# Linear attention and an MLP mixer: attention on pairs of chunks, two-bank units, and an issue order planned in the kernel

## The chip, the cores and the metric

One core of a Trainium2 chip. The metric is the device time of one execution in microseconds (us).

Names: PE is TensorE (matmul), DVE is VectorE, ACT is ScalarE, POOL is GpSimd, SP is SyncE, which here only starts transfers. "ch1" and "ch2" are the two channel matmuls of the mixer, "tok1" and "tok2" the two token matmuls. PSUM is the memory, in banks, into which the matmuls of these kernels write; an eviction is the pass of VectorE or ACT that takes a result out of it. The granted clock is the share of its full clock that TensorE was given (PEclk in the views).

## The reference

Four batches, eight heads, 768 times, head size 48; then a mixer over times and channels.

```
f = 1 / (1 + exp(-f_logit))
for t in range(S):
    state = f[:, :, t, :, None] * state + outer(k[t], v[t])
    y[:, :, t] = q[t] @ state
x = y as [B, S, 384]
h = relu(x^T @ w_tok1) @ w_tok2            # 768 -> 256 -> 768, over times
u = x + h^T
out = u + relu(u @ w_ch1) @ w_ch2          # 384 -> 1536 -> 384, over channels
```

## The kernel before

It does attention one chunk of 128 times at a time. Gates are cumulative sums of log f, made by a matmul with a triangle; q and k are gated, transposed on TensorE, multiplied to scores, masked, and multiplied with v; a state is carried on. The mixing of batch b is cut into six slices, issued in the gaps of attention of batch b+1. Loads that also cast to bf16 are started by POOL:

```python
def load_batch_inputs(b, c0=0, c1=NCH):          # cut
    for c in range(c0, c1):
        nc.sync.dma_start(out=f_sb[i][:, :, c, :], in_=f_logit[b]...)
        nc.gpsimd.dma_start(out=q_sb[i][:, :, c, :], in_=q[b]...)   # and k, v
```

```python
# in attn_chunk(b, c); HP = 4 pairs of heads; cut
nc.vector.tensor_tensor(qh[i][:, :, 0:D], q_sb[ib][:, :, c, :], G[i][:, :, 0:D], ALU.mult)
nc.vector.tensor_tensor(kh[i][:, :, 0:D], k_sb[ib][:, :, c, :], Gi[i][:, :, 0:D], ALU.mult)
for hp in range(HP):
    nc.tensor.matmul(ps_AT[0][:, hp, :], lhsT=qb[:, hp, :], rhs=ident, start=True, stop=True)
for hp in range(HP):
    nc.tensor.matmul(ps_AT[1][:, hp, :], lhsT=kb[:, hp, :], rhs=ident, start=True, stop=True)
nc.scalar.copy(qkT[i][:, 0:4, :], ps_AT[0])
nc.vector.tensor_copy(qkT[i][:, 4:8, :], ps_AT[1])
# ... scores, mask, times v, state
```

```python
# in s_ch (ch1), evictions of 384 columns, one PSUM bank; cut
nc.tensor.matmul(pm[:, 0:384], lhsT=w_ch1[:, kt, cc * 128:(cc + 1) * 128],
                 rhs=uT[:, kt, th * 384:(th + 1) * 384], start=(kt == 0), stop=(kt == 2))
```

## Time and profile before

| kernel before | |
|---|---|
| time | 242.1 us median (242.0 to 242.7) |
| span of the profile | 240.4 us |
| TensorE busy, matmuls | 183.6 us, 1688 (by the weight loads; 15 matmul records are missing) |
| VectorE, ACT, POOL busy | 152.1, 137.2, 40.1 us |
| first ch1 matmul | 83.9 us |

The page of the kernel before: busy time, share of the span and instruction count of each engine, then TensorE's busy tenths in 40 slices of the span.

```profile
span 240.4 us, 4273 instructions
PE 183.6 (76%) x1673; PEld 111.5 (46%) x1688; DVE 152.1 (63%) x341; ACT 137.2 (57%) x262; POOL 40.1 (17%) x39
PE   0413376103858999999999999999999999989993
```

TensorE is nearly full from slice 14 on and mostly idle in the first ten. The table by stretches shows both stages; each row has the stretch, its length, and for each engine the busy time and the number of instructions, then the granted clock:

```profile
20.00:44.00 24.00, 11.86 (x108) 7.49 (x110) 17.75 (x32) 23.35 (x29) 10.84 (x8) 1.00 3.00 151
44.00:58.00 14.00, 0.70 (x12) 0.48 (x11) 1.06 (x3) 4.50 (x6) 5.67 (x6) 1.00 2.52 167
119.00:163.00 44.00, 41.99 (x417) 25.84 (x421) 34.51 (x83) 24.36 (x60) 1.39 (x1) 1.00 0.33 42
```

From 44 to 58 us TensorE does 0.7 us of work; later it does 42 of every 44. The chain that ended last (start, length, what) says what filled the head:

```profile
6.98 15.19 DMA q_sb_77<-in_q_dram
...
28.49 2.21 POOL k_sb_80 L78
30.70 11.26 issue
41.96 1.73 POOL v_sb_82 L79
44.17 13.95 DMA w_tok_73<-in_moe_w_tok_dram
```

POOL's queue holds the loads of batch 1 in front of the weights of the mixing. The load of v of batch 1 waits 11 us, so the weights are issued at 44 and are there at 58.

### The profile page before, as it was taken

The page shows a single profiled execution, that of the slowest core. Times are in us where ns is not written, and L with a number is a line of the kernel's source. Part 1 is how long each engine was busy: PE and PEld are TensorE (multiplying, and loading weights), DVE is VectorE, ACT ScalarE, POOL GpSimd, SP SyncE. Part 2 cuts the span into 40 slices and gives each one's busy share as a digit, 9 for nine tenths or more (in the row PEclk, how much of TensorE's full clock was granted, in tenths as well). Part 3 has the DMA queues.
Part 4 walks back from the last instruction along what each step waited for, and adds up shares of the span by engine and source line. Part 5 has one row for each costly group of instructions (what it writes and reads, how often), then busy time and mean ns, then how long its engine had stood idle before and what let it go on. Part 6 is the DMA issues. An engine that isn't in the chain of part 4 may idle for free.

```text
span 240.4 us, 4273 instructions
## 1 busy us (share of the span) xinstructions
PE 183.6 (76%) x1673; PEld 111.5 (46%) x1688; DVE 152.1 (63%) x341; ACT 137.2 (57%) x262; POOL 40.1 (17%) x39
## 2 busy tenths in 40 slices
PE   0413376103858999999999999999999999989993
PEld 0201253001535555566565555666556556546661
DVE  4323769300965999995489998637999872444221
ACT  5479999900697765870376777008776710556300
POOL 9823910821302100150300000000000000000000
PEclk9999999999965999999999999999999999999999
DMA  8999999999999900099490000121000002100022
GB/s 113 147 185 151 163 158 137 174 144 198 208 182 137 103 3 0 3 85 174 135 104 0 3 1 3 65 100 35 0 3 0 3 33 102 64 0 0 8 107 85
DMA packets 91539, 19.93 MB, mean 83 GB/s; under 512 B 80896, under 2 KB 91136, under 8 KB 91520
## 3 DMA queue, kind: packets, MB, share of 16 engines
q0 software_dynamic: 77168, 10.23, 78.3%
q1 hardware_dynamic: 14352, 9.44, 18.4%
q8 instruction: 13, 0.21, 0.4%
q14 instruction: 6, 0.05, 0.1%
HBM read 25.17 MB, written 4.72 MB: 124 GB/s over the span
## 4 chain that ended last, share of the span: by engine, by line
PE 34%; DVE 26%; DMA 15%; issue 9%; ACT 8%; POOL 7%; DVEq 0%; POOLq 0%
DMA q_sb_77<-in_q_dram 6%; DMA w_tok_73<-in_moe_w_tok_dram 6%; PE ps_moe_135 L298 5%; PE ps_moe_133 L298 5%; PE ps_moe_134 L298 5%; PE ps_moe_133 L280 3%; DMA out_dram<-out_sb_132 3%; DVE zT L285 3%; PE ps_moe_134 L280 3%; PE ps_moe_135 L280 3%; DVE u_nat L256 2%; DVE qkT_98 L186 2%; DVE AmT_99 L200 2%; DVE uT L270 2%; DVE state L225 2%
## 5 line engine op out<-in xcount | busy, mean ns | idle before, releaser
L298 PEld LDWEIGHTS <-zT 128*128 128x128 bf16 x288 | 27.7, 98 | 18.3
L280 PEld LDWEIGHTS <-w_ch_75 128*128 128x128 bf16 x288 | 26.5, 97 | 19.9 <-issue 4.5
L280 PE MATMUL ps_moe_133<-uT,w_ch_75 128*128 128x384 bf16 x96 | 22.9, 325 | 1.4 <-DVE uT L270 0.5
L280 PE MATMUL ps_moe_135<-uT,w_ch_75 128*128 128x384 bf16 x96 | 22.6, 325 | 0.8 <-DVE zT L285 0.5
L280 PE MATMUL ps_moe_134<-uT,w_ch_75 128*128 128x384 bf16 x96 | 22.2, 325 | 0.5 <-DVE zT L285 0.3
L220 ACT ACTIVATE x_nat_105<-ps_y 128x384 f32<-128x384 f32 x12 | 6.0, 499 | 24.8 <-PE ps_y L210 24.2
L298 PE MATMUL ps_moe_134<-w_ch_76,zT 128*128 128x384 bf16 x96 | 17.3, 326 | 0.0
L200 DVE TENSOR_TENSOR AmT_100<-ps_AT_122,tri_bf 128x512 bf16<-128x512 f32 x12 | 8.3, 688 | 14.2 <-PE ps_AT_123 L191 14.0
L298 PE MATMUL ps_moe_135<-w_ch_76,zT 128*128 128x384 bf16 x96 | 17.1, 326 | 0.0
L298 PE MATMUL ps_moe_133<-w_ch_76,zT 128*128 128x384 bf16 x96 | 17.1, 326 | 0.0
L287 ACT ACTIVATE zT<-ps_moe_134 128x384 bf16<-128x384 f32 x22 | 10.9, 496 | 8.0 <-PE ps_moe_134 L280 7.8
L161 PE MATMUL ps_dg<-ones_bf,Lhi_85 128*128 128x1 bf16 x40 | 3.5, 166 | 13.5 <-ACT Lhi_85 L143 6.7
L287 ACT ACTIVATE zT<-ps_moe_135 128x384 bf16<-128x384 f32 x22 | 11.0, 500 | 4.9 <-PE ps_moe_135 L280 4.8
L220 ACT ACTIVATE x_nat_104<-ps_y 128x384 f32<-128x384 f32 x12 | 5.8, 486 | 13.9 <-PE ps_y L210 13.9
L247 PE MATMUL ps_moe_134<-x_bf_106,w_tok_73 128*128 128x384 bf16 x6 | 2.5, 452 | 14.1 <-DMA w_tok_73<-in_moe_w_tok_dram 12.2
L247 PEld LDWEIGHTS <-w_tok_73 128*128 128x128 bf16 x48 | 4.6, 105 | 17.9 <-DMA w_tok_73<-in_moe_w_tok_dram 12.4
L287 ACT ACTIVATE zT<-ps_moe_133 128x384 bf16<-128x384 f32 x20 | 10.0, 500 | 4.3 <-PE ps_moe_133 L280 4.2
L224 DVE TENSOR_TENSOR state<-state,ps_dg 48x192 f32<-48x192 f32 x20 | 6.8, 342 | 8.5 <-ACT qkT_98 L185 4.9
L257 ACT ACTIVATE u_bf<-u_nat 128x384 bf16<-128x384 f32 x24 | 11.0, 519 | 1.8 <-DVE u_nat L256 1.6
L200 DVE TENSOR_TENSOR AmT_99<-ps_AT_122,tri_bf 128x512 bf16<-128x512 f32 x12 | 8.2, 685 | 6.0 <-PE ps_AT_123 L191 5.7
L175 ACT ACTIVATE glast<-ps_dg 128x4 f32<-128x4 f32 x20 | 3.6, 178 | 14.1 <-DVE state L227 12.7
L191 PE MATMUL ps_AT_122<-qkT_97 48*128 48x128 bf16 x48 | 5.1, 232 | 7.3 <-ACT qkT_97 L185 5.5
(149 smaller groups left out, 470.3 us busy)
## 6 DMA issues: line engine op xcount, KB each, us to landing
out_dram<-out_sb_131 SPq DMA_DIRECT2D x12, 192.0 KB, 1.9
out_dram<-out_sb_132 SPq DMA_DIRECT2D x12, 192.0 KB, 1.9
f_sb_83<-in_f_logit_dram SPq DMA_DIRECT2D x6, 192.0 KB, 5.7
q_sb_78<-in_q_dram POOLq DMA_DIRECT2D x2, 576.0 KB, 12.6
k_sb_80<-in_k_dram POOLq DMA_DIRECT2D x2, 576.0 KB, 18.2
v_sb_82<-in_v_dram POOLq DMA_DIRECT2D x2, 576.0 KB, 11.6
w_ch_75<-in_moe_w_ch_dram POOLq DMA_DIRECT2D x1, 1152.0 KB, 20.3
w_ch_76<-in_moe_w_ch_dram POOLq DMA_DIRECT2D x1, 1152.0 KB, 24.9
```

The source lines that it names most:

```text
L186: nc.vector.tensor_copy(qkT[i][:, 4:8, :], ps_AT[1])
L191: nc.tensor.matmul(ps_AT[par][:, hp, :], lhsT=qkT[i][rows, 4 + hp, :], rhs=qkT[i][rows, hp, :], start=True, stop=True)
L200: nc.vector.tensor_tensor(AmT[i][:, 0:4, :], ps_AT[0], tb4, ALU.mult)
L220: nc.scalar.activation(x_nat[ib][:, c, :], yflat, AF.Copy, bias=0.0, scale=1.0)
L224: nc.vector.tensor_tensor(state[0:D], state[0:D], ps_dg[0:D, :, 0:D], ALU.add)
L225: nc.vector.tensor_tensor(state[64:64 + D], state[64:64 + D], ps_dg[64:64 + D, :, D:2 * D], ALU.add)
L247: nc.tensor.matmul(pm[:, 0:DM], lhsT=w_tok1[:, kt, rt * 128:(rt + 1) * 128], rhs=x_bf[ib][:, kt, :], start=(kt == 0), stop=(kt == NCH - 1))
L257: nc.scalar.activation(u_bf[:, stt, :], u_nat[:, stt, :], AF.Copy, bias=0.0, scale=1.0)
L280: nc.tensor.matmul(pm[:, 0:384], lhsT=w_ch1[:, kt, cc * 128:(cc + 1) * 128], rhs=uT[:, kt, th * 384:(th + 1) * 384], start=(kt == 0), stop ...
L285: nc.vector.tensor_scalar(dst, pm[:, 0:384], 0.0, None, ALU.max)
L287: nc.scalar.activation(dst, pm[:, 0:384], AF.Relu, bias=0.0, scale=1.0)
L298: nc.tensor.matmul(pm[:, 0:DM], lhsT=zT[:, kt, tt * 128:(tt + 1) * 128], rhs=w_ch2[:, kt, :], start=(kt == 0), stop=(kt == 11))
```

## The change

The intent: half as many small instructions in attention (times 2p and 2p+1 on partition p, so one cumulative sum serves two chunks), passes of 768 or 1024 columns over two PSUM banks instead of 384 or 512, transposes on the DMA engines instead of TensorE for q, k and u of batches 1 to 3, fp32 loads on SP's queue with the casts on POOL, and one order for everything. That order is made by a planner inside the kernel: every operation has an assumed duration and a priority; the planner simulates the engines, picks engine and buffer greedily, and issues in the order that it found. Each engine then runs its instructions strictly in that order. The diff, cut to its core (constants, imports and most of the planner left out):

```diff
+LD_ISSUE, ROW = 0.8, 0.019 / 16
+class Planner:
+    # greedy: of the ready operations, the one with the earliest start, then the
+    # lowest prio; (occupancy, latency) of each engine it may run on is given
+    ...
+                    cand = [s for s in self.pools[p] if s[1] is not None and s[1] <= st + 1e-9]
+                    s = max(cand, key=lambda s: s[1])
+XB_FROM = 1
-        nc.gpsimd.dma_start(out=q_sb[i][:, :, c, :], ...)
+        P.op(f"ld{nm}{b},{d}", {"SP": (LD_ISSUE, 0)}, [], [f"{nm}{b},{d}"],
+             lambda: nc.sync.dma_start(out=P[f"{nm}{b},{d}"]..., in_=src[d]), ...)
-    nc.gpsimd.dma_start(out=w_tok2, in_=moe_w_tok2.rearrange("(kt p) n -> p kt n", p=128))
+    P.op("w2", {"DVE": (1.0, 0.1)}, ["w2s0", "w2s1"], ["w2"], lambda: [nc.vector.tensor_copy(
+        w_tok2[:, kt].rearrange("r c (two p) -> r c p two", two=2), ...) for kt in range(2)], -898)
+            nc.gpsimd.tensor_copy(o[0:64, 0:2], x[0:64])          # v cast, one of four
-    for hp in range(HP):
-        nc.tensor.matmul(ps_AT[0][:, hp, :], lhsT=qb[:, hp, :], rhs=ident, start=True, stop=True)
+        xbar = b >= XB_FROM
+        if not xbar:
+            # batch 0: 16 transposes of a pair on TensorE, evicted 1024 columns at a time
+            ...
+        else:
+            for e in range(2):
+                P.op(f"xb_t{i},{e}", {"ACT": (0.8, 0)}, [f"qh{i}", f"kh{i}"], [f"qkT{i},{e}"],
+                     lambda e=e: nc.scalar.dma_start_transpose(
+                         P[f"qkT{i}"][:, 1024 * e:1024 * (e + 1)]..., P[f"qh{i}"][64 * e:64 * e + 64]),
+                     pr - 500, xfer=-1.1)
+            # u, batches 1 to 3:
+                P.op(f"uT{i}", {"ACT": (1.0, 0)}, [f"ub{i}"], [f"uT{i}"],
+                     lambda i=i, p=p: nc.scalar.dma_start_transpose(...), p_tok - 500, xfer=-0.8)
+    for s, _, o, e in P.order:       # issue in the planned order
+        o.fn(e)
```

The numbers in parentheses after an engine are the durations that the planner assumes: 0.8 us of ACT for starting a q/k transpose, 1.0 for one of u, 0.8 of SP for a load.

## The prediction

> **What bounds the kernel now.** Two stages. Until 58.2 us nothing of the mixing runs. The chain of waits shows why: q/k/v pieces issued one after another from POOL (about 0.9 us each, a 15.2 us DMA step), an 11.3 us "issue" wait in POOL's queue behind the batch-1 loads, then w_tok1, issued at 44.2 and landed 13.9 us later. The table by stretches gives PE 16.3 us busy of the first 58. From 58 to 237 TensorE is the limit: 41.5 to 42 us busy of each 43 to 44 us per batch, DVE 34 to 36, ACT 24. (58 to 76 also ran at a granted clock of 0.76.) From matmul spacing in the timeline (0.163 us at 384 columns, 0.22 at 512, 0.055 for a 128-column transpose, 0.026 to 0.045 for the small ones) TensorE needs about 27.4 us per batch for the mixing and 2.4 us per chunk for attention: 170 us in all, 156 of them in those 179 us, so 87% used. After that stage only a 0.55 us add and a store remain.
>
> **What the change does.**
> 1. Attention on pairs of times: half the cumulative sums, gate sums and score/AV groups. I count 2.1 to 2.4 us TensorE per two chunks instead of 4.8. Transposes of q/k (batches 1 to 3) and u go to DMA. TensorE total: 109 mixing + 27 attention + 4 transposes of batch 0 = 140 us, 30 less.
> 2. Two-bank evictions of 768 or 1024 columns. From the trace a DVE pass costs 0.15 us + 1.04 ns per column, ACT 0.19 + 0.83 ns, so DVE about 127 us of 152. ACT about 80 us of 137, plus 27 transpose issues of 1 to 1.7 us that hold its queue; the nine act-table loads of 1.28 us become one.
> 3. Casting loads leave POOL: q/k/v/f are fp32 on the SP queue with 384-byte rows instead of 192; POOL casts v, state and x. w_tok1 is issued once k of the second pair landed, not after batch 1.
> 4. Planned order interleaves attention b+1 with mixing b.
>
> **On the critical path.** Head: twelve 393 KB loads at 1.3 to 2.5 us each, first pair's chain about 15 us after f lands at 4, then DVE bound in batch 0 (about 8.5 us per pair by the formula above) for two more pairs: x complete near 36, tokens, u and its transpose near 43 instead of about 81. Only about 16 us of TensorE work is done by then. The remaining 124 us, at about 93% use, take 134. Tail 3.5: a 0.95 us add, two stores. Sum about 180 of span; the time reads 1.7 us above the span.
>
> **Prediction: 181 us, 8 in 10 between 171 and 195.** Faster by over 2%: 0.97; within 2%: 0.02; slower: 0.01.
>
> **What would show it.** First ch1 matmul at 40 to 46 us; TensorE at least 90% busy from there to the end; TensorE matmul count 1514; no DMA wait for weights over 3 us; DVE around 125 us busy, ACT 80.
>
> **What would make it wrong.** DMA transposes: no trace here has one. The Trainium skill, "DMA: Bandwidth & Descriptors", Latency and other measured facts, puts them at 261 GB/s, so 1 us per 256 KB is an estimate; slower ones, or ACT held while issuing, delay scores and ch1 (u's transposes sit between tokens and channels in every batch). POOL as caster: "SBUF — State Buffer", Who interferes with whom, says a DVE instruction with two SBUF inputs blocks GpSimd reads; the gates are such, and POOL produces v and state. Loads and weights (11 MB) competing at the start could push ch1 past 50. A fixed order that guesses durations wrongly makes engines wait in line. All push up; better interleaving pushes to 172.

## The result, and the profile after

The kernel after takes 234.1 us median (232.6, 232.7, 235.5, 235.6). The ratio to the kernel before is 0.965, 95% interval 0.959 to 0.971. Ratios in this document compare the runs of two kernels in the same rounds, and are not quite the ratio of the medians quoted. It is faster, and 53 us slower than predicted, far outside the range.

| | before | predicted | after |
|---|---|---|---|
| time, us | 242.1 | 181 | 234.1 |
| TensorE matmuls | 1688 | 1514 | 1514 |
| first ch1, us | 83.9 | 40 to 46 | 58.0 |
| VectorE busy, us | 152.1 | 125 to 127 | 145.1 |
| ACT busy, us | 137.2 | 80 and 27 issues | 90.4 and 49.4 of issues |

The page of the kernel after, as that of before:

```profile
span 230.7 us, 3882 instructions
PE 172.3 (75%) x1514; PEld 101.9 (44%) x1514; DVE 145.1 (63%) x221; ACT 90.4 (39%) x130; POOL 84.0 (36%) x134
PE   0455726585976859948828999929998999799990
PEclk9999999999795999995965999988999999999998
DMA  7999999999897999979990330693435004711052
```

TensorE starts earlier but then has holes (a 4, two 2s, a 7 after the first third), where before it was at 9 throughout; between slices 11 and 28 the granted clock falls at times as well. The table by stretches of the kernel after (same columns as before):

```profile
60.00:80.00 20.00, 15.66 (x146) 8.27 (x145) 15.47 (x25) 13.77 (x21) 9.22 (x15) 0.77 1.06 214
80.00:100.00 20.00, 17.23 (x164) 10.29 (x163) 16.19 (x20) 8.32 (x13) 15.00 (x21) 1.00 1.03 203
100.00:120.00 20.00, 11.51 (x119) 6.40 (x118) 12.19 (x18) 5.66 (x8) 4.87 (x9) 0.75 1.04 194
140.00:160.00 20.00, 15.78 (x132) 8.85 (x130) 12.01 (x23) 5.81 (x10) 5.05 (x10) 0.91 0.52 83
200.00:220.00 20.00, 20.00 (x125) 12.05 (x124) 5.74 (x6) 6.49 (x8) 0.00 (x0) 1.00 0.13 32
```

From 100 to 120 no engine computes for more than 61% of the time: TensorE 11.5 of 20, VectorE 12.2, ACT 5.7. ACT's queue is held by issues for about 11 more, which the table does not count as busy. This is not a load that is too big but engines waiting for one another. The transfers (what, who starts them, how many, KB each where known, median us from issue to landing):

```profile
qkT<-qkh ACTq DMA_TRANSPOSE x18, 4.7
uT<-u_bf ACTq DMA_TRANSPOSE x9, 2.8
```

ACT's own timeline from 99 us on shows what such a transpose does to it. ACTq is ACT's queue held by an issue, not ACT computing; in brackets the idle time before and what ended it:

```profile
98.99 3.12 ACTq L421 DMA_TRANSPOSE qkT<-qkh  x2
102.16 0.81 ACT L377 ACTIVATE G<-pp 128x768 bf16<-128x768 f32 x1 [7.01 <-issue]
102.87 0.81 ACT L379 ACTIVATE Gi<-pp 128x768 bf16<-128x768 f32 x1
103.56 0.84 ACT L346 ACTIVATE f_ld<-f_ld 128x768 f32<-128x768 f32 x1
104.44 0.84 ACT L348 ACTIVATE f_ld<-f_ld 128x768 f32<-128x768 f32 x1
105.19 0.79 ACT L533 ACTIVATE h1T<-pp 128x768 bf16<-128x768 f32 x1
105.87 4.50 ACTq L421 DMA_TRANSPOSE qkT<-qkh  x2
```

The gate exponentials of line 377 stand behind two transposes. At 145 us four transposes in a row hold ACT for 7.7 us, and TensorE's token matmul waits 4.2 us for the eviction that stands behind them (the last line is TensorE's timeline):

```profile
145.47 7.67 ACTq L421 DMA_TRANSPOSE qkT<-qkh  x4
153.18 0.81 ACT L533 ACTIVATE h1T<-pp 128x768 bf16<-128x768 f32 x1 [7.68 <-issue]
154.04 1.10 PE L548 MATMUL pp<-h1T,w_tok 128*128 128x384 bf16 x4 [4.22 <-ACT h1T L533]
```

The issue of one q/k transpose took (minimum, median, maximum in ns, then first and last start):

```profile
L421 ACTq DMA_TRANSPOSE qkT<-qkh x18: 1257/1758/3676, 57.6 to 172.7; - x18
```

The planner assumes 800. The pieces of ACTq in the timeline sum to 49.4 us. SP is touched too: the waits of SP's queue have its loads waiting for transposes, because in the compiled program the transfers of SP and ACT take eight completion semaphores in turn, and a transfer waits until an earlier user of its semaphore has landed (what waited, for what: us in total, times, longest):

```profile
SPq L258 <- DMA qkT<-qkh: 27.2, 5, 7.5
```

So there are three suspects in the transposes: ACT held while it issues, the time to landing that the scores wait for, and the traffic and semaphores shared with the loads. The chain of waits of this kernel has all of them. Two landings stand in it:

```profile
80.54 8.19 DMA qkT<-qkh
107.16 5.27 DMA qkT<-qkh
```

Landings of q/k transposes are 5.8% of this chain (13 us) and their issues on ACT 3.8% (9 us).

The head is a second loss. Up to 58 us VectorE is busy 44.4 us, and 17.8 of the 20 between 20 and 40. The loads do not hold it: the only one in the chain of waits before 58 us is the first of f, 3.9 us. Two things on VectorE took longer than estimated, the two copies that permute w_tok2 (planner: 1.0 us for both) and the gates, and batch 1's gates had a bad place in the order:

```profile
L288 DVE COPY w_tok<-zT x2: 2240/2388/2537, 26.2 to 28.0; 128x768 bf16<-128x768 bf16 x2
```

```profile
53.69 1.65 DVE L398 TENSOR_TENSOR qkh<-q_ld,G 128x384 bf16<-128x384 f32 x2
55.26 2.27 DVE L398 TENSOR_TENSOR qkh<-k_ld,Gi 128x384 bf16<-128x384 f32 x2
57.45 0.94 DVE L576 CAST uT<-pp 128x768 bf16<-128x768 f32 x1
```

The second fence is VectorE's timeline just before the first ch1: the last eviction of batch 0's transposed u, which ch1 needs, stands behind the gates of batch 1. TensorE had made that transpose by 55.5.

### The profile page after: what moved, and what is told of

The parts are those of the page before. It is cut to its first block, busy times and chain, and to the rows that moved or that the text cites. A ratio compares the mean times of both kernels' runs of the same rounds, so it can differ in the third digit from the quotient of the medians.

```text
span 230.7 us, 3882 instructions
## 1 busy us (share of the span) xinstructions
PE 172.3 (75%) x1514; PEld 101.9 (44%) x1514; DVE 145.1 (63%) x221; ACT 90.4 (39%) x130; POOL 84.0 (36%) x134
## 3 DMA queue, kind: packets, MB, share of 16 engines
q10 hardware_dynamic: 26208, 6.49, 19.2%
## 4 chain that ended last, share of the span: by engine, by line
PE 41%; DVE 19%; DMA 15%; ACT 9%; issue 8%; ACTq 4%; POOL 1%; SPq 0%; DVEq 0%; POOLq 0%
PE pp L595 15%; PE pp L626 12%; DVE qkh L398 7%; DMA qkT<-qkh 6%; DVE AmT L454 4%; ACTq L421 4%; PE pp L548 3%; DMA q_ld<-in_q_dram 3%; DMA out_dram<-xu 3%; PE pp L528 2%; PE pp L451 2%; DVE state L493 2%; DMA uT<-u_bf 2%; ACT xu L510 2%; ACT f_ld L346 2%
## 5 line engine op out<-in xcount | busy, mean ns | idle before, releaser
L595 PE MATMUL pp<-uT,w_ch 128*128 128x384 bf16 x288 | 58.6, 348 | 5.9 <-ACT zT L606 2.2
L626 PE MATMUL pp<-w_ch,zT 128*128 128x384 bf16 x288 | 57.2, 331 | 2.1 <-ACT xu L510 1.9
L595 PEld LDWEIGHTS <-w_ch 128*128 128x128 bf16 x288 | 28.0, 103 | 26.9 <-issue 11.0
L606 ACT ACTIVATE zT<-pp 128x768 bf16<-128x768 f32 x31 | 24.7, 813 | 32.3 <-PE pp L595 27.4
L454 DVE TENSOR_TENSOR AmT<-pp,msk 128x1024 bf16<-128x1024 f32 x24 | 28.9, 1220 | 9.7 <-PE pp L451 9.4
L506 POOL CAST state_bd<-state 48x192 bf16<-48x192 f32 x40 | 15.8, 396 | 34.4 <-DVE state L496 27.5
L608 DVE TENSOR_SCALAR zT<-pp 128x768 bf16<-128x768 f32 x17 | 16.3, 957 | 15.3 <-PE pp L595 11.7
L638 DVE TENSOR_TENSOR xu<-xu,pp 128x768 f32<-128x768 f32 x12 | 11.4, 949 | 19.0 <-PE pp L626 19.0
L554 DVE TENSOR_TENSOR xu<-xu,pp 128x768 f32<-128x768 f32 x12 | 11.2, 952 | 13.6 <-PE pp L548 13.6
L398 DVE TENSOR_TENSOR qkh<-q_ld,G 128x384 bf16<-128x384 f32 x24 | 15.1, 670 | 4.3 <-ACT G L377 4.3
L398 DVE TENSOR_TENSOR qkh<-k_ld,Gi 128x384 bf16<-128x384 f32 x24 | 17.7, 776 | 0.0
L302 POOL CAST x_bf<-xu 128x768 bf16<-128x768 f32 x10 | 8.5, 846 | 25.3 <-ACT xu L510 22.6
L451 PEld LDWEIGHTS <-qkT 48*128 48x128 bf16 x192 | 7.2, 110 | 16.2 <-issue 8.7
```

Of the source, the lines that this page charges most:

```text
L398: nc.vector.tensor_tensor(gated(z, nm, j), x[:, j], gg[:, j], ALU.mult)
L451: nc.tensor.matmul(A[:, par, hp], lhsT=qkT(1, hp, e, rows), rhs=qkT(0, hp, e, rows), start=True, stop=True)
L454: P.op(f"mk{ic}", {"DVE": dve_t(1024)}, [f"A{ic}"], [f"Am{ic}"], lambda ic=ic: nc.vector.tensor_tensor(P[f"Am{ic}"], P[f"A{ic}"].rearrange ...
L506: nc.gpsimd.tensor_copy(P[f"bd{ic}"][r, :, cl], P[f"st{ic}"][r])
L595: nc.tensor.matmul(pm[:, th, 0:384].rearrange("p (a t) -> p a t", t=128), lhsT=w_ch1[:, kt, cc * 128:(cc + 1) * 128], rhs=uT[:, 3 * th:3 * ...
L606: nc.scalar.activation(o, x, AF.Relu)
```

## The experiments

The theory: the DMA transposes cost the time between the first ch1 and the end, by holding ACT and by landing late. The rivals: it is not the transposes but an order made from wrong durations, whatever the operation; buffers handed out too soon; or the head alone, whose delay the rest only carries on.

All kernels are built from the kernel after by the edit shown. The planner runs again in each, so where durations or engines are edited the order on all engines changes too; where that is not so, it is said. Every run gave a correct result and was timed in three rounds. They were timed in five sets on five chips; the median of the kernel before lay between 242.2 and 242.9 us in all of them. Two more builds never ran, because the greedy planner found no order: a2 with the planner told that SP issues the transposes, and d1 without the later priority of the copies.

| run | time, us (median) | ratio to before | 95% interval |
|---|---|---|---|
| after | 234.1 | 0.965 | 0.959 to 0.971 |
| a1_no_xbar | 218.0 | 0.898 | 0.895 to 0.901 |
| a2_sp_xbar | 226.8 | 0.935 | 0.932 to 0.939 |
| a3_fifo | 230.0 | 0.947 | 0.945 to 0.950 |
| a4_replan | 224.4 | 0.923 | 0.919 to 0.926 |
| b1_u_xbar | 218.0 | 0.898 | 0.895 to 0.901 |
| b2_w2_on_act | 216.6 | 0.893 | 0.891 to 0.895 |
| b3_v_on_act | 222.0 | 0.914 | 0.912 to 0.917 |
| n1_null | 233.1 | 0.961 | 0.955 to 0.967 |
| c1_dummy_xbar | 239.3 (mean of three) | 0.988 | 0.981 to 0.995 |
| c2_dummy_on_sp | 224.4 | 0.925 | 0.921 to 0.929 |
| c3_hold_act | 236.4 | 0.971 | 0.966 to 0.976 |
| d1_costs_tensor | 215.1 | 0.889 | 0.887 to 0.891 |
| d2_costs_u_dma | 212.0 | 0.875 | 0.873 to 0.877 |
| d3_costs_fifo | 213.8 | 0.883 | 0.880 to 0.885 |
| d4_best_fifo | 212.7 | 0.878 | 0.873 to 0.882 |
| e2_ev_on_act | 211.1 | 0.870 | 0.866 to 0.874 |

### a1: all transposes on TensorE

```diff
-    XB_FROM = 1
+    XB_FROM = 4
```

> All transposes of batches 1 to 3 (q, k and u) back on TensorE with evictions on ACT and DVE; the planner makes a new order. Theory 1 (the DMA transposes, 49 us of ACT's queue and 4.7 us median to landing, cost most of the missing 50 us): TensorE gets about 11 us more work and still the kernel gets faster, 205 to 222 us. Theory 2 (early reuse of buffers, and waits between queues): 230 to 240. Theory 3 (DVE and POOL slower than planned by contention): 235 or more, since DVE gets more work.

Measured: 218.0 us, 16 under the kernel after, with 198 matmuls more. The page of a1, TensorE's line and its slices:

```profile
PE 174.3 (81%) x1712; PEld 109.7 (51%) x1712; DVE 148.8 (69%) x224; ACT 114.1 (53%) x157; POOL 81.7 (38%) x131
PE   0456536659668689979987999999899999999990
PEclk9999999999979999999999999999999999999999
```

The holes after 100 us are gone and the clock is at full speed but for one slice. The DMA transposes took more than the TensorE work they were to save. First ch1 is at 58.7, as before the edit: the head has nothing to do with them.

### b1: only q and k back on TensorE

```diff
-        xbar = b >= XB_FROM
+        xbar = False
```

> Only the nine u transposes stay DMA transposes; q and k are transposed on TensorE in all batches. If the 18 q/k transposes are the cost (34 us of ACT's queue, scores wait for them): near the kernel without any, 215 to 221 us. If the u transposes between tokens and channels cost as much: 222 to 230.

Measured: 218.0 us, the same as a1. So the nine transposes of u by DMA cost nothing net in this plan; the 18 of q and k are the whole difference.

### a2: the transposes issued from SP

```diff
-  nc.scalar.dma_start_transpose(        # both places
+  nc.sync.dma_start_transpose(
```

The order on TensorE, VectorE and POOL is exactly that of the kernel after.

> The same plan and order on PE, DVE, ACT and POOL, only the 27 transposes are issued by SP instead of ACT. If it is the time ACT is held while issuing (49 us in all): 210 to 222 us. If it is the latency of the transposes or the plan: 228 to 238, and the loads and stores behind them in SP's queue may come later.

Measured: 226.8 us; 7 of the 16 us came back. The waits of a2 show where the rest went: the loading of score weights, and the score matmuls, wait for the transposes, up to 10 us at a time.

```profile
PEld L451 <- DMA qkT<-qkh: 18.8, 6, 10.2
PE pp L451 <- DMA qkT<-qkh: 16.6, 4, 9.8
```

SP's queue is in order as well, so transposes and loads now hold each other up there. This run alone cannot divide the cost.

### a3: buffers taken first in, first out

```diff
-                    s = max(cand, key=lambda s: s[1])
+                    s = min(cand, key=lambda s: s[1])
```

The order on all engines is that of the kernel after; only which buffer is used changes.

> Same order on every engine; only the choice of a free buffer is changed from the most recently freed to the longest free. Theory 2 (ACT at 116 us waits for a store of a tile that was reused although others were free, loads wait for just-used tiles): 220 to 228 us. Theories 1 and 3: 230 to 235.

Measured: 230.0 us. Taking the buffer freed last, which the planner believes free, makes 4 us of waits where its times are wrong: a small term.

### a4: the planner told what the trace shows

```diff
-    LD_ISSUE, ROW = 0.8, 0.019 / 16
+    LD_ISSUE, ROW = 1.4, 0.019 / 16
-    P.op("w2", {"DVE": (1.0, 0.1)}, ...
+    P.op("w2", {"DVE": (4.4, 0.1)}, ...
-                P.op(f"xb_t{i},{e}", {"ACT": (0.8, 0)}, ...
+                P.op(f"xb_t{i},{e}", {"ACT": (1.8, 0)}, ...
-                P.op(f"uT{i}", {"ACT": (1.0, 0)}, ...
+                P.op(f"uT{i}", {"ACT": (1.3, 0)}, ...
```

> Same instructions, replanned with the issue times that the trace shows: 1.8 us per q/k transpose, 1.3 per u transpose, 1.4 per load, 4.4 for the w_tok2 permutation. If a fixed order made from wrong durations is the loss: 212 to 225 us. If the transposes cost in themselves: 226 to 236.

Measured: 224.4 us, 10 us better with the same operations. So part of the loss is that the order was made with wrong durations. This run corrects four of them at once, so it does not show how much of the 10 us belongs to that of the q/k transposes, told at less than half the true one. And it is not the whole loss: a4 is still 6 us above b1, which kept the wrong durations and only took the q/k transposes off the DMA engines.

### n1: a shuffled plan, nothing else

A changed plan could be better or worse by luck. This run changes one assumed latency and thereby the order.

```diff
-PE_LAT = 0.10
+PE_LAT = 0.15
```

> A control: the changed kernel with one planner constant nudged (0.10 to 0.15 us), which shuffles the order without making it truer. Says how far any new order moves the time. 230 to 237 us if the order is not the matter; outside that, differences of that size between replanned kernels prove nothing.

Measured: 233.1 us, within the spread of the kernel after. This shuffle moved the time by about 1 us, so gains of 10 and 16 are unlikely to be luck. It is one shuffle only; a difference of 3 us between two plans is less safe.

### c1, c2, c3: which part of a q/k transpose costs

All three are a1 (the scores read transposes made by TensorE) plus something that nobody reads. They share one plan, and the order on TensorE, VectorE and POOL is the same in all three (c2 has one more memset at the start).

```diff
# c1: 18 DMA transposes into unread tiles, started by ACT
+    P.op(f"xb_t{i},{e}", {"ACT": (0.8, 0)}, [f"qh{i}", f"kh{i}"], [],
+         lambda e=e: nc.scalar.dma_start_transpose(dummy..., P[f"qh{i}"][64 * e:64 * e + 64]), ...)
# c2: the same from SP, reading a fixed tile: traffic only
+         lambda e=e: nc.sync.dma_start_transpose(dummy[0]..., dummy[1][64 * e:64 * e + 64]), ...)
# c3: ACT held by a copy of 1900 columns: no transfer
+         lambda e=e: nc.scalar.copy(dummy[e][:, 0:1900], P[f"qh{i}"][:, 0:1900]), ...)
```

> As a1 (scores read q/k transposed by TensorE), plus the 18 q/k DMA transposes of batches 1 to 3 issued from ACT into tiles that nobody reads. a1 read 218.0. If the cost of the q/k transposes is that they hold ACT's queue (18 times about 1.8 us) and slow the loads, this run keeps it: 225 to 232, with ACT-queue steps in the chain of waits and PE waiting for ACT evictions. If the cost is that the scores wait for the transposes' results (4.7 us to land), this run loses it: 218 to 221. From the run with the transposes on SP (7 of 16 us gone) I expect between: about 224, and no PE wait on DMA qkT.

Measured: 239.3 us (mean of three runs, 237.2 to 240.5). My expectation of 224 was wrong: nobody waits for the results any more, and the whole cost is still there and more, 21 us over a1. The wait of the scores for the landing is therefore not needed to explain it.

> c1 with the 18 unread DMA transposes issued from SP and reading a fixed tile, so they hold no ACT and wait for no data; order on PE, DVE and POOL is that of c1. What is left of them is their traffic and their time and semaphores in SP's queue among the loads. If that was c1's cost: 232 to 239. If holding ACT was it: 218 to 222. I expect 221.

Measured: 224.4 us, 6 over a1. Traffic, SP's time, semaphores and the different plan cost that much together.

> c1 with each of the 18 unread DMA transposes replaced by an ACT copy of 1900 columns (about 1.75 us by the copies in the trace) into an unread tile: ACT is held as long as by a median issue, no transfer, no DMA semaphore. If the bare holding of ACT is the cost: 230 to 238. If the cost of the issues is their waiting in ACT's queue for a DMA completion semaphore still in use by a load, or the transfers: 219 to 224. I expect about 228.

Measured: 236.4 us, 18 over a1, without a single transfer. A copy takes 1776 ns (c3), an issue 1800 in median (c1, slow run):

```profile
L405 ACT COPY dummy<-qkh x18: 1758/1776/1779, 57.9 to 179.5; 128x1900 bf16<-128x1900 bf16 x18
```

```profile
L405 ACTq DMA_TRANSPOSE dummy<-qkh x18: 1257/1800/3211, 57.0 to 182.6; - x18
```

Holding ACT for that time, 18 times, at places where the plan left 0.8 us, is most of the cost: c1 is 15 us above c2, and c3, without any transfer, is 12 above c2, which has the same plan, and 18 above a1, which has another. Holding here includes standing in the queue: in c3 ACT also waited 7.0 us, four times, for the gates that the copy reads, and nothing waited for the copies' results. ACT is busy only 58% of c3's span, so it is not overloaded. What it does next is late, and everything behind stands in order. The table by stretches, a1 first and then c3:

```profile
58.00:100.00 42.00, 35.61 (x378) 21.89 (x377) 38.97 (x60) 30.68 (x45) 26.20 (x39) 0.96 0.94 205
```

```profile
58.00:100.00 42.00, 34.33 (x338) 20.83 (x339) 35.29 (x50) 34.75 (x43) 26.22 (x39) 0.80 0.68 154
```

TensorE started 378 matmuls in this stretch in a1 and 338 in c3, and both VectorE and TensorE are less busy. TensorE's granted clock is lower too, 0.80 against 0.96, so a part of the loss comes through the clock. A caveat: in c1 and c3 ACT also evicts TensorE's transposes, which it doesn't in the kernel after. So these are shares in c1, not measured in the kernel after.

### b2 and b3: the head

b2 is a1 with the two w_tok2 copies on ACT at the same place in the order; b3 also puts the v casts of batch 0 on ACT instead of POOL.

```diff
# b2
-    P.op("w2", {"DVE": (1.0, 0.1)}, ..., lambda: [nc.vector.tensor_copy(
+    P.op("w2", {"DVE": (1.0, 0.1)}, ..., lambda: [nc.scalar.copy(
# b3, in addition
-            nc.gpsimd.tensor_copy(o[0:64, 0:2], x[0:64])      # and three more
+            cp = nc.scalar.copy if b == 0 else nc.gpsimd.tensor_copy
+            cp(o[0:64, 0:2], x[0:64])
```

> The kernel without DMA transposes (217.97 us), same order on all engines, only the two permuting copies of w_tok2 (2.39 us each on DVE, in the DVE-bound head, beside POOL's casts) are issued on ACT. If the head is DVE bound and they lie on its path: 3 to 5 us less, 213 to 215. If the head waits for something else: 217 to 219.

Measured: 216.6 us, 1.4 under a1, first ch1 at 56.4 instead of 58.7. On ACT the two copies took 7.1 us and held up an eviction that TensorE waited 3.9 us for, with VectorE behind it (2.9 us), so most of the gain was probably given back there.

> As the last, and in batch 0 the four casts of v per pair go from POOL to ACT, same order. If POOL's reads slow DVE's two-input instructions (gates 0.67 to 0.97 us where 0.5 is seen alone): gates in the first 58 us fall to 0.55 and the kernel gains 2 to 4 us more, 209 to 213. If ACT then lies on the path: 214 to 218.

Measured: 222.0 us, worse than b2 by 5: a miss. But it settles one thing. The timelines of VectorE, the gates of batch 0's first two pairs, b2 and then b3:

```profile
10.16 1.65 DVE L398 TENSOR_TENSOR qkh<-q_ld,G 128x384 bf16<-128x384 f32 x2 [0.29 <-ACT G L377]
11.74 1.95 DVE L398 TENSOR_TENSOR qkh<-k_ld,Gi 128x384 bf16<-128x384 f32 x2
20.02 1.16 DVE L398 TENSOR_TENSOR qkh<-q_ld,G 128x384 bf16<-128x384 f32 x2
21.10 1.79 DVE L398 TENSOR_TENSOR qkh<-k_ld,Gi 128x384 bf16<-128x384 f32 x2
```

```profile
10.14 1.03 DVE L399 TENSOR_TENSOR qkh<-q_ld,G 128x384 bf16<-128x384 f32 x2 [0.29 <-ACT G L377]
13.92 1.03 DVE L399 TENSOR_TENSOR qkh<-k_ld,Gi 128x384 bf16<-128x384 f32 x2 [2.75 <-ACT Gi L379]
21.27 1.02 DVE L399 TENSOR_TENSOR qkh<-q_ld,G 128x384 bf16<-128x384 f32 x2
22.21 1.02 DVE L399 TENSOR_TENSOR qkh<-k_ld,Gi 128x384 bf16<-128x384 f32 x2
```

Two gates take 1.02 us when POOL is not casting and up to 1.95 when it is. The Trainium skill, "SBUF — State Buffer", Who interferes with whom, has VectorE and GpSimd share one pair of ports under an exclusive lock; these lines agree that casts slow the gates, and do not show a lock as such. In b3 ACT held the head up instead: TensorE waited 6.3 us at one place for an eviction behind the copies and casts on ACT, and VectorE 6.7 us behind it.

### d1 to d4: combinations

d1 is a1 with the measured durations (1.4 us per load issue, 4.4 us for w_tok2's copies) and the copies at a priority behind batch 0's masks. d2 is d1 with u's transposes by DMA (1.3 us told), q and k on TensorE. d3 and d4 are d1 and d2 with buffers first in, first out.

```diff
# d2 against the kernel after
-    LD_ISSUE, ROW = 0.8, 0.019 / 16
+    LD_ISSUE, ROW = 1.4, 0.019 / 16
-    P.op("w2", {"DVE": (1.0, 0.1)}, ..., -898)
+    P.op("w2", {"DVE": (4.4, 0.1)}, ..., 62)
-        xbar = b >= XB_FROM
+        xbar = False
-                P.op(f"uT{i}", {"ACT": (1.0, 0)}, ...
+                P.op(f"uT{i}", {"ACT": (1.3, 0)}, ...
```

> All transposes on TensorE as in a1, planner told the measured 1.4 us per load issue and 4.4 us for the two w_tok2 copies, which also get a priority behind batch 0's mask passes (in the planner 62 instead of -898). If mis-told durations still cost time without any DMA transpose: 213 to 216. If a1's remaining loss is only work (DVE in the head): 217 to 219. First ch1 at 55 to 57 against 58.7 in a1.

> The same measured costs, q/k on TensorE, the nine u transposes by DMA and told at 1.3 us. b1 read the same as a1, so theory says the same as d1 within 1 per cent: 212 to 217. TensorE count about 1658.

> d1 with the buffer that was freed longest ago taken instead of the one freed last; instruction order as d1. The same change was worth 4 us in the after kernel, where buffers were held by late transposes. If buffer reuse makes engines wait without them too: 2 to 4 us under d1; if it only mattered for late transposes: within 1 us of d1.

> d2 (q/k on TensorE, u by DMA, measured durations; 212.0) with the buffer freed longest ago taken, which was worth 1.3 us on d1. 210 to 212 if the same here.

Measured: d1 215.1, d2 212.0, d3 213.8, d4 212.7. Measured durations, with the copies placed later, are worth 3 us on a1 and 6 on b1. The buffer rule is worth 1.3 us on d1 and nothing on d2. d2 is 3 us under d1: with q and k on TensorE, moving u's transposes to the DMA engines may gain a little, though the plans differ and b1 gained nothing on a1. It is 9% under the kernel after and 12.5% under the kernel before.

### e2: less work for VectorE

In d2 VectorE is busy 42.1 of the 44.5 us from the first ch1 to 100 us (the third figure with a count):

```profile
55.50:100.00 44.50, 38.88 (x422) 23.88 (x419) 42.09 (x63) 31.17 (x46) 25.95 (x39) 0.98 1.06 221
```

e2 lets only ACT evict the transposed q/k of batches 1 to 3.

```diff
-  P.op(f"ev{z}{i}", {"ACT": act_t(1024), "DVE": dve_t(1024)}, ...
+  P.op(f"ev{z}{i}", {"ACT": act_t(1024)} if b else {"ACT": act_t(1024), "DVE": dve_t(1024)}, ...
```

> d2 with the evictions of transposed q/k of batches 1 to 3 allowed on ACT alone; VectorE gets about eight instructions fewer, some 8 to 10 us. If VectorE, not TensorE, limits the stretch from the first ch1 to about 100 us (39.8 of 42 us busy in d2): TensorE use rises there and the time falls by 2 to 5 us, to 207 to 210. If TensorE or ACT limits it: within 1.5 us of 212.

Measured: 211.1 us; the interval of its ratio overlaps that of d2, so it isn't shown to be faster. It is also a poor test: VectorE lost 8.5 us over the whole span, but only 1.8 of them in the stretch in question. That VectorE limits this stretch remains a reading of the table, not a result.

## Why the prediction was wrong

The busy time of TensorE is no measure of work: a ch1 matmul lasts 0.326 us in the trace, but back to back they start every 0.1625 us. For the sums below, work is the number of matmuls of each kind in a stretch times the spacing that the trace shows when they run back to back (0.1625 us for 384 columns, 0.055 for a transpose, 0.0255 to 0.042 for the small ones).

**The work was right.** Predicted 140 us in all, 16 before the first ch1 and 124 after it. Counted in the trace of after: 16.2 and 125.5. The matmul count, 1514, was exact. The sum, 141.7, is within 2 us of the prediction.

**The head: 43 predicted, 58.0 measured (+15).** The step that failed is "x complete near 36, tokens, u and its transpose near 43". The last x of batch 0 was complete near 45.7: VectorE, which I had named as the limit, had 4.8 us of permuting w_tok2 that I had left out, and gates and sums slowed by POOL's casts (in b2's trace the six pairs of gates of batch 0 sum to 8.6 us where 6 times 1.03 would be 6.2). I had cited the port rule as a risk and given it no microseconds. From 45.7 to 58 instead of 7 us it took 12, with the gates of batch 1 in front of the last eviction. No run shows that these terms are the 15 us: with the copies elsewhere, b2 and d1 bring the first ch1 only to 56.4 and 55.6, so the cause of most of the head's loss stays open. VectorE's total, 145 instead of about 126, comes in part from the same terms: the 48 gates took 32.8 us, 6 more than at 0.55 us each; w_tok2 adds 4.8; the sums of line 350 averaged 0.79 us. The remainder I have not divided.

**The stage: 134 us at 93% use predicted, 166.7 measured (+33).** From 58.0 to the last matmul's end at 224.7, 125.5 us of work is 75% use. The step that failed is "The remaining 124 us, at about 93% use, take 134", through the term "27 transpose issues of 1 to 1.7 us that hold its queue", which I had added to ACT's load and not to any wait. The issues took 49.4 us of ACT's queue, 1.8 each in the mean. ACT's load with them, 140 us of 231, looked harmless, and it was not the load that mattered. In a1, with no such issue, the same stage takes 152.4 us for 135.6 us of work: 89% use. So 14 of the 18 points of use that were missing go with the DMA transposes, and b1 puts them on the 18 of q and k. c1, c2 and c3 show one mechanism that is enough to make such a loss: ACT held in an in-order queue, with no landing awaited. In the kernel after itself landings are awaited too (13 us of its chain against 9 of issues), so there the division stays open. The clock follows: 0.75 in the stretch where TensorE idled most, nearly full speed in a1. The Trainium skill, "TensorE: Matmul & The Clock Gate", Part 1, says that the clock drops after TensorE has idled; the traces agree in part. In the kernel before, TensorE works 0.7 of 14 us from 44 to 58 at a clock of 1.00, and the drop to 0.76 comes in the 18 us after. It is part of the loss: in the stage of after the clock is at half for 30.6 us, in five stretches, and TensorE is busy in 22.6 of them, so about 11 us more than at full clock is an estimate; in a1 it is 3.4 us, so under 2. No run separates this from the waits that bring it on.

**The transfer rate.** The prediction took "1 us per 256 KB" from the Trainium skill, "DMA: Bandwidth & Descriptors", Latency and other measured facts (261 GB/s effective for a DMA transpose with a non-contiguous middle dimension), and warned that "ACT held while issuing" could make it wrong. Landing took 4.7 us in median. The warning named the mechanism that c3 shows; the range did not hold it. Counting the 27 issues at their upper figure of 1.7 us would have given 46 us, close to the measured 49.4, so the duration was not the main error: the error was to let a wait in an in-order queue be absorbed.

**The tail: 3.5 predicted, 6.0 measured** (last matmul's end at 224.7 to the end of the span).

The three differences, 15, 33 and 2.5, make the 50 us between the predicted sum of 180.5 and the span of 230.7. What the profile should show was stated well: the first ch1 and "at least 90% busy" (85% from 58.0 to 224.7) both failed and pointed at the head and at the stage; the count held.

**What stays open.** How the loss in the kernel after itself divides between holding ACT, landings, semaphores and the clock is not measured; c1 to c3 show the first in another plan. Also open is the limit of d2 from 55 to 100 us, where VectorE is 95% busy and the loads are running at 221 GB/s at the same time. Between d2 and the predicted span lie 30 us. By the same count of work they are 12.5 in the head (55.5 for 43), about 8 for the 144 transposes that are back on TensorE, about 7 for 88% use instead of 93%, and 2.6 in the tail; this division is an estimate from counts and spacings, not an experiment.

## What to carry to other kernels

Price an issue that holds an engine's queue by what stands behind it, not by its share of the engine's time: ACT was busy 58% of the span in c3, and 18 unread copies of 1.8 us still cost 12 us against c2 and 18 against a1. If the issue order is fixed by assumed durations, read those durations from a trace of the kernel itself and plan again (10 us here, with no other change), and include null shuffles, more than the one made here, so that luck is not taken for a gain. Before moving work off a busy engine, ask what the new place serialises: here 198 transposes on TensorE were cheaper than 27 on the DMA engines.

## What the Trainium skill lacked or had wrong

- "DMA: Bandwidth & Descriptors", Issuing engines are not separate DMA queues: it calls the time to initiate a DMA "usually small relative to the DMA itself". For a q/k DMA transpose here the issue held ACT for 1.76 us in median, against 4.7 us from issue to landing, and 18 unread issues went with 21 us of kernel time (c1 over a1, another plan included). The page gives sequencer cycles for transposes of earlier generations, in a passage on trn3, and no issue time for one of this size on trn2.
- Same page, Latency and other measured facts: 261 GB/s effective for DMA transposes with a non-contiguous middle dimension. In the kernel after, the queue that carries the transposes moved 6.49 MB in 19.2% of the span as time of all 16 engines, which is 44 us, so about 147 GB/s by this estimate, beside loads.
- "SBUF — State Buffer", Who interferes with whom: the rule fits what these runs show and has no size for this case. Two 128x384 gates took 1.02 us alone and up to 1.95 us beside POOL's casts (b2, b3).
- No page that I used warns that transfers of SP and ACT may take completion semaphores in turn, so that a load waits for the landing of another engine's transpose: 27.2 us of waiting in SP's queue, five times.
